# Spreading the fp8 matmuls of a q-k product over a step, and turning inverse norms into a row by way of DRAM

## The chip, the cores and the metric

One core of one Trainium2 chip. The metric is the device time of one execution in microseconds (us); medians over several runs are quoted. The kernel before takes 815.4 us.

Engines: PE is TensorE's matmuls, PEld its weight loads, DVE is VectorE, ACT is ScalarE, POOL is GpSimd, SP is SyncE. L12 is line 12 of the kernel in question.

## The reference

```python
B, N, C = 4, 6016, 256
qn = q / (norm(q, axis=1) + 1e-6)             # over N, one norm for each of 256 columns
kn = k / (norm(k, axis=1) + 1e-6)
a  = softmax(kn.T @ qn / tau, axis=-1)        # 256 x 256 for each of 4 batches
x  = (v @ a).reshape(B * N, 256)
out = (silu(x @ w_gate) * (x @ w_val)) @ w_out     # 24064 tokens, 256 -> 1536 -> 256
```

The kernel folds `a` into the two large weights (Wg, Wv: 256 x 1536 a batch), so that the tokens need three products only: g, v and o.

## The kernel before

Its main loop has 576 steps: 4 batches of 12 chunks of 512 tokens (the last of 384), each with 12 slices of 128 hidden columns. A step puts two matmuls of 512 columns into g, two into v and four of 256 columns into o. During the steps of one batch, the attention of the next is prepared in the background, by a plan that says what is added at which of 144 steps.

```python
    def gemm1_pair(b, t):                      # two slabs of 128 rows of q and k
        ...
        for jh in range(CH):                   # CH = 2
            js = slice(jh * P, (jh + 1) * P)
            if pm == 2:
                nc.tensor.matmul(kq[:, jh, :], q_sb[:, ps:ps + 2, js],
                                 k_sb[:, ps:ps + 2, :], ..., perf_mode=DR)
            else:                              # the 47th slab stands alone
                nc.tensor.matmul(kq[:, jh, :], q_sb[:, ps, js], k_sb[:, ps, :], ...)
    ...
    def norm_cols(b):
        ...                                    # column sums, then inverse norms in inv
        parts = split3(inv[:, CH:], [P, CH], "ink")      # three bf16 parts
        ...
    def norm_diag(b):                          # six diagonal matrices, on DVE
        ...
    def norm_rows(b):                          # ones x diagonal = a row on every partition
        for i in range(3):
            nc.tensor.matmul(ps, ones_bf, state[b, "diag"][:, i], start=(i == 0), stop=(i == 2))
        ink = work.tile([P, C], FP32, tag="ink")
        nc.vector.tensor_copy(ink, ps)
    ...
    def logits(b, jh):                         # DVE: kq * inverse norm of q * row of k
        ...
    plan[step + 1].append((gemm1_pair, t))     # both fp8 matmuls at the end of a step
    ...
    plan[S1 + 10].append((norm_cols,))         # S1 = 82
    plan[S1 + 20].append((norm_diag,))
    plan[S1 + 22].append((norm_rows,))
    plan[S1 + 24].append((logits, 0))
```

DoubleRow (`DR`) multiplies two fp8 slabs at once. The first batch is prepared before the loop, in another way that the change doesn't touch.

## Time and profile before

| | before |
|---|---|
| median of 3 runs | 815.44 us (815.43 to 816.31) |
| span of the profiled run | 813.6 us |
| PE busy | 98% |
| DVE, ACT, POOL busy | 65%, 53%, 33% |
| clock granted to TensorE | 1.0 |

The span starts with the first instruction, so it is a little shorter than the time. A matmul's record overlaps the next one's (one of 512 columns is recorded as 0.38 us, and the next starts 0.216 us after it), so busy shares hide small losses. The distance between the starts of successive g products (the length of a step) does not, and the argument rests on it. The lines stand in the prediction.

### The profile page before, as it was taken

How to read it: one execution, taken by the hardware profiler on the slowest of the kernel's cores; microseconds unless marked ns; L12 is line 12 of the kernel's file. 1: busy time of each engine (PE TensorE's matmuls, PEld its weight loads, DVE VectorE, ACT ScalarE, POOL GpSimd, SP SyncE). 2: the span in 40 equal slices, each digit the busy share in tenths (PEclk: the TensorE clock that was granted, in tenths of full speed). 3: DMA queues.
4: the chain of work that ended last, by engine and by line, in shares of the span. 5: the costliest groups of instructions: out<-in, count | busy, mean ns of one | idle time of the engine just before them, and what ended most of it. 6: DMA issues, size and time to landing. Idle time of an engine off the chain costs nothing.

```text
span 813.6 us, 13772 instructions
## 1 busy us (share of the span) xinstructions
PE 800.4 (98%) x5037; PEld 487.1 (60%) x5037; DVE 526.7 (65%) x816; ACT 434.9 (53%) x756; POOL 265.8 (33%) x344
## 2 busy tenths in 40 slices
PE   5999999999999999999999999999999999999998
PEld 3656666665565666666565666666656565665666
DVE  4777777667556777756756687765765555555554
ACT  4566655545555656545555556654554544444543
POOL 5515887313000888722000388751300000000000
PEclk9999999999999999999999999999999999999999
DMA  9993875328311678333812368632652112112101
GB/s 88 143 158 69 112 105 88 78 53 122 80 40 46 96 100 105 74 65 88 127 40 59 53 87 118 92 78 66 141 97 66 46 48 57 53 39 65 50 27 59
DMA packets 93220, 64.59 MB, mean 79 GB/s; under 512 B 52593, under 2 KB 92017, under 8 KB 92401
## 3 DMA queue, kind: packets, MB, share of 16 engines
q0 software_dynamic: 19200, 27.01, 28.6%
q1 hardware_dynamic: 73952, 36.71, 17.7%
q8 instruction: 39, 0.64, 0.3%
q14 instruction: 29, 0.23, 0.1%
HBM read 78.64 MB, written 36.70 MB: 142 GB/s over the span
## 4 chain that ended last, share of the span: by engine, by line
PE 95%; DMA 4%; POOL 1%; issue 0%; DVE 0%; POOLq 0%
PE o_new L463 30%; PE g_ps L429 30%; PE v_ps L429 30%; PE ps L398 2%; PE kq_new L149 2%; DMA v_sb<-in_v_dram 1%; DMA k_sb<-in_k_dram 1%; DMA q_sb<-in_q_dram 1%; POOL k_sb L104 1%; PE ps L331 0%; PE unit_ps L398 0%; PE cs L305 0%; PE kq_new L154 0%; PE ps L388 0%; PE vt_ps L128 0%
## 5 line engine op out<-in xcount | busy, mean ns | idle before, releaser
L439 DVE TENSOR_TENSOR sv<-silu,v_ps 128x512 bf16<-128x512 bf16 (+1 forms) x576 | 388.6, 675 | 263.2 <-ACT silu L435 261.4
L435 ACT ACTIVATE silu<-g_ps 128x512 bf16<-128x512 f32 (+1 forms) x576 | 338.6, 588 | 324.6 <-PE g_ps L429 302.0
L463 PE MATMUL o_new<-w_out_sb,sv 128*128 128x256 bf16 x2256 | 338.3, 273 | 0.0
L429 PE MATMUL g_ps<-vT,Wg 128*128 128x512 bf16 (+1 forms) x1128 | 331.1, 375 | 0.0
L429 PE MATMUL v_ps<-vT,Wv 128*128 128x512 bf16 (+1 forms) x1128 | 330.4, 374 | 0.0
L463 PEld LDWEIGHTS <-sv 128*128 128x128 bf16 x2256 | 220.7, 98 | 140.8
L429 PEld LDWEIGHTS <-Wv 128*128 128x128 bf16 x1152 | 112.7, 98 | 130.8 <-ACT Wv L410 0.2
L281 POOL TENSOR_TENSOR acc_new<-acc_new,sq 128x512 f32<-128x512 f32 x135 | 157.3, 1165 | 43.7 <-DVE sq L271 33.7
L429 PEld LDWEIGHTS <-Wg 128*128 128x128 bf16 x1152 | 106.7, 98 | 27.0 <-ACT Wg L410 0.2
L271 DVE TENSOR_TENSOR sq<-q_sb 128x512 bf16<-128x512 fp8e5 x72 | 63.9, 888 | 0.0
L276 POOL TENSOR_TENSOR acc_new<-sq 128x512 f32<-128x512 bf16 x3 | 3.5, 1152 | 150.7 <-DVE sq L271 150.7
L272 ACT ACTIVATE sq<-k_sb 128x512 bf16<-128x512 fp8e5 x72 | 44.2, 614 | 0.0
L149 PE MATMUL kq_new<-k_sb,q_sb 128*128 128x512 fp8e5 x184 | 40.0, 309 | 0.7 <-DMA q_sb<-in_q_dram 0.7
L472 ACT COPY o_sb<-o_new 128x512 f32<-128x512 f32 x48 | 28.1, 586 | 14.9 <-PE o_new L463 14.5
L474 DVE COPY o_sb<-o_new 128x512 f32<-128x512 f32 (+1 forms) x48 | 31.8, 661 | 3.0 <-PE o_new L463 3.0
L104 POOL DMA_DIRECT2D q_sb<-in_q_dram x48 | 27.0, 562 | 13.3 <-DMA k_sb<-in_k_dram 5.4
L104 POOL DMA_DIRECT2D k_sb<-in_k_dram x48 | 26.0, 549 | 11.3 <-DMA w_out_sb<-in_moe_w_out_dram 5.3
L176 PE MATMUL ss_new<-sq,ones_bf 128*128 128x256 bf16 x83 | 17.6, 351 | 9.0 <-ACT sq L166 8.4
L112 POOL DMA_DIRECT2D vb<-in_v_dram x47 | 24.1, 516 | 5.3 <-DMA vb<-in_v_dram 3.2
L149 PEld LDWEIGHTS <-q_sb 128*128 128x256 fp8e5 x184 | 22.1, 138 | 3.1 <-DMA q_sb<-in_q_dram 2.3
L176 PEld LDWEIGHTS <-ones_bf 128*128 128x128 bf16 x83 | 9.8, 121 | 15.7 <-issue 11.4
L351 POOL TENSOR_SCALAR den<-th 128x512 f32<-128x512 f32 x3 | 1.8, 612 | 51.8 <-ACT th L350 51.8
(93 smaller groups left out, 201.7 us busy)
## 6 DMA issues: line engine op xcount, KB each, us to landing
out_dram<-o_sb SPq DMA_DIRECT2D x92, 256.0 KB, 2.4
vb<-in_v_dram POOLq DMA_DIRECT2D x43, 256.0 KB, 5.4
k_sb<-in_k_dram POOLq DMA_DIRECT2D x44, 128.0 KB, 5.8
q_sb<-in_q_dram POOLq DMA_DIRECT2D x44, 128.0 KB, 5.0
w_out_sb<-in_moe_w_out_dram POOLq DMA_DIRECT2D x1, 768.0 KB, 13.5
vb<-in_v_dram POOLq DMA_DIRECT2D x4, 192.0 KB, 3.5
vT<-vb SPq DMA_TRANSPOSE x47, 3.8
w_gate_sb<-in_moe_w_gate_dram POOLq DMA_DIRECT2D x2, 256.0 KB, 7.3
```

The lines of the kernel that those rows point to most:

```text
L104: nc.gpsimd.dma_start(out=dst[:, gs:gs + gm, :], in_=src[b].rearrange("(p s) c -> p s c", s=NS)[:, gs:gs + gm, :])
L149: nc.tensor.matmul(kq[:, jh, :], q_sb[:, ps:ps + 2, js], k_sb[:, ps:ps + 2, :], start=(t == 0 and jh == 0), stop=last, perf_mode=DR, skip_ ...
L176: nc.tensor.matmul(state[b, "ss", which], ones_bf, sq[:, s, :], start=(t == 0 and s == 0), stop=(t == t_last and s == pm - 1))
L271: nc.vector.tensor_mul(sq[:, :pm, 0, :], q_sb[:, ps:ps + pm, :], q_sb[:, ps:ps + pm, :])
L272: nc.scalar.activation(sq[:, :pm, 1, :], k_sb[:, ps:ps + pm, :], ACT.Square)
L281: nc.gpsimd.tensor_tensor(out=acc, in0=acc, in1=sq[:, s, :, :], op=ALU.add)
L429: nc.tensor.matmul(dst[:, :mv], W[:, kk, fs], vT[:, kk, :mv], start=(kk == 0), stop=(kk == CH - 1))
L435: nc.scalar.activation(silu[:, :mv], g_ps[:, :mv], ACT.Silu)
L439: nc.vector.tensor_mul(sv[:, f, :mv], silu[:, :mv], v_ps[:, :mv])
L463: nc.tensor.matmul(self.o_ps[:, j % 2, :], self.sv[:, f, j * P:(j + 1) * P], w_out_sb[:, f, :], start=(f == 0), stop=(f == FH - 1))
L472: nc.scalar.copy(o_sb[:, :m, :], self.o_ps[:, :m, :])
L474: nc.vector.tensor_copy(o_sb[:, :m, :], self.o_ps[:, :m, :])
```

## The change

Its intent: to put something of 512 columns between the two fp8 matmuls of a pair, so that their long weight loads are hidden, and to take the nine diagonal matmuls off PE.

```diff
-        plan[step + 1].append((gemm1_pair, t))
+        pair_at[step + 1] = t
...
-        for dst, W in ((g_ps, Wg), (v_ps, Wv)):
+        for n, (dst, W) in enumerate(((g_ps, Wg), (v_ps, Wv))):
             for kk in range(CH):
                 nc.tensor.matmul(dst[:, :mv], W[:, kk, fs], vT[:, kk, :mv], ...)
+            if pair is not None:
+                gemm1_pair(b + 1, pair, (n,))
...
-        parts = split3(inv[:, CH:], [P, CH], "ink")
-        ... (norm_diag and norm_rows go)
+        row = dram.tile([C], FP32, tag="ink_row")
+        nc.gpsimd.dma_start(out=row.rearrange("(h p) -> p h", p=P), in_=inv[:, CH:])
         ink = work.tile([P, C], FP32, tag="ink")
-        nc.vector.tensor_copy(ink, ps)
+        nc.gpsimd.dma_start(out=ink, in_=row.partition_broadcast(P))
```

A pair's step now reads g, fp8, v, fp8, o.

More of the change, by code (lines that the diff above doesn't have):

```diff
@@ L135, in evacuate_first_v, with gemm1_pair @@
         nc.vector.tensor_copy(vt_ready[(0, 0)][:, h, :], state["vt_ps"][:, h, :])
-    def gemm1_pair(b, t):
+    def gemm1_pair(b, t, jhs=range(CH)):
         q_sb, k_sb = qk_tiles[b]
-        if t == 0:
+        if t == 0 and 0 in jhs:
             kq_new = psum_kq.tile([P, CH, C], FP32, tag="kq")
@@ L145, in gemm1_pair @@
         last = t == NP - 1
-        for jh in range(CH):
+        for jh in jhs:
             js = slice(jh * P, (jh + 1) * P)
@@ L312, in norm_cols @@
         state[b, "inv"] = inv
-        parts = split3(inv[:, CH:], [P, CH], "ink")
-        scal = work.tile([P, 3, CH], FP32, tag="scal")
-        for i, part in enumerate(parts):
-            nc.gpsimd.tensor_copy(scal[:, i, :], part)
-        state[b, "scal"] = scal
-    def norm_diag(b):
-        scal = state[b, "scal"]
-        diag = work.tile([P, 3, CH, P], BF16, tag="diag")
-        for i in range(3):
-            for h in range(CH):
-                nc.vector.tensor_scalar_mul(diag[:, i, h, :], in0=ident,
-                                            scalar1=scal[:, i, h:h + 1])
-        state[b, "diag"] = diag
-    def norm_rows(b):
-        ps = psum_m.tile([P, C], FP32, tag="misc")
-        for i in range(3):
-            nc.tensor.matmul(ps, ones_bf, state[b, "diag"][:, i], start=(i == 0),
-                             stop=(i == 2))
+        row = dram.tile([C], FP32, tag="ink_row")
+        nc.gpsimd.dma_start(out=row.rearrange("(h p) -> p h", p=P), in_=inv[:, CH:])
         ink = work.tile([P, C], FP32, tag="ink")
-        nc.vector.tensor_copy(ink, ps)
+        nc.gpsimd.dma_start(out=ink, in_=row.partition_broadcast(P))
         state[b, "ink"] = ink
@@ L417, in wp_unit, with gv_matmuls @@
         wp_evacuate(b, u, ps, part, u % 2 == 1 if on_dve is None else on_dve)
-    def gv_matmuls(b, ci, f):
+    def gv_matmuls(b, ci, f, pair=None):
         cs, cm = chunks[ci]
@@ L479 @@
     plan = [[] for _ in range(STEPS)]
+    pair_at = {}
     for g in range(len(groups)):
@@ L489 @@
     plan[S1 + 10].append((norm_cols,))
-    plan[S1 + 20].append((norm_diag,))
-    plan[S1 + 22].append((norm_rows,))
     plan[S1 + 24].append((logits, 0))
@@ L560 @@
         for f in range(FH):
-            g_ps, v_ps, mv = gv_matmuls(b, ci, f)
+            pair = pair_at.get(ci * FH + f) if b + 1 < B else None
+            g_ps, v_ps, mv = gv_matmuls(b, ci, f, pair)
             us = range(2 * f + 2, min(2 * f + 4, len(wp_units))) if gi == 0 else ()
```

## The prediction

> **What bounds the kernel now.** I read the page first: the span, the busy shares, the chain that ended last.
>
> ```profile
> span 813.6 us, 13772 instructions
> PE 800.4 (98%) x5037; PEld 487.1 (60%) x5037; DVE 526.7 (65%) x816; ACT 434.9 (53%) x756; POOL 265.8 (33%) x344
> PE 95%; DMA 4%; POOL 1%; issue 0%; DVE 0%; POOLq 0%
> ```
>
> The first 36 us are loads; after that everything on the chain is PE. A busy PE is not yet a PE at its pace, so I read the timeline of PE next (start, length, work) and took the distance between the g products of successive steps.
>
> ```profile
> 54.13 0.59 PE L429 MATMUL g_ps<-vT,Wg 128*128 128x512 bf16 x2
> ...
> 64.53 0.59 PE L429 MATMUL g_ps<-vT,Wg 128*128 128x512 bf16 x2
> ...
> 67.35 0.61 PE L429 MATMUL g_ps<-vT,Wg 128*128 128x512 bf16 x2
> ...
> 95.22 0.60 PE L429 MATMUL g_ps<-vT,Wg 128*128 128x512 bf16 x2
> ...
> 101.53 0.60 PE L463 MATMUL o_new<-w_out_sb,sv 128*128 128x256 bf16 x4
> 101.88 0.46 PE L149 MATMUL kq_new<-k_sb,q_sb 128*128 128x512 fp8e5 x2
> 102.19 0.61 PE L429 MATMUL g_ps<-vT,Wg 128*128 128x512 bf16 x2
> 102.63 0.59 PE L429 MATMUL v_ps<-vT,Wv 128*128 128x512 bf16 x2
> ```
>
> From 54.13 to 64.53 lie eight steps without q-k work: 10.40/8 = 1.300 us each. A step streams 4 x 512 + 4 x 256 = 3072 columns, so this is 0.42 ns a column with all included: about 0.216 us for a 512-wide matmul and 0.109 us for a 256-wide one. Stepping through the whole timeline, I found no step between 50 us and the end that is longer than what its matmuls add up to, except as told below. So PE is at its pace, nothing it waits for is worth anything, and only two things can move the time: matmuls taken off PE, and columns that cost more than 0.42 ns.
>
> **What the Trainium skill says.** (1) "Perfetto Trace Analysis", section Identifying the Most-Contended Engine, warns that the matmul busy share does not tell the distance to the limit; hence the steps above, and not the 98%. (2) "TensorE: Matmul & The Clock Gate", section Back-to-back issue gap, gives N/2.4 + 2.5 ns, which is 215.8 and 109.2 ns for 512 and 256 columns; the trace agrees (0.216, 0.109). (3) The same page, section Weight-path perf modes, says that DoubleRow fp8 switches the fast weight load off and makes a weight load 72% dearer. The trace has this smaller, 138 against 98 ns (the groups of weight loads, fp8 128x256 against bf16 128x128). (4) "DMA: Bandwidth & Descriptors", section Anatomy of one DMA, gives about 2.0 us fixed for a transfer issued from GpSimd, mostly the receipt of the last byte. The trace shows 2.4 us for the output stores, issued from SyncE, and 5.4 us for the v loads of 256 KB.
>
> **Part 1: the fp8 matmuls.** What does a pair (two DoubleRow matmuls of 256 columns) cost now? From 67.35 to 95.22 are 20 steps with eight pairs: 27.87 - 20 x 1.300 = 1.87 us, 0.234 us a pair. Two 256-wide matmuls at pace are 0.218. Only 0.016 us a pair is excess. So the most that any new place for these matmuls can win is 0.016 us x 69 pairs (three hidden batches of 23 DoubleRow pairs; the 24th is a single slab without DoubleRow) = 1.1 us, 0.14% of the time. Their own columns are not saved by moving them.
>
> Where does the excess sit? The 138 ns weight load, longer than the 109 ns matmul that should hide it, is the first suspect. It is not the culprit. In the timeline of the weight loads:
>
> ```profile
> 100.56 0.21 PEld L429 LDWEIGHTS <-Wg 128*128 128x128 bf16 x2
> ...
> 101.86 0.25 PEld L149 LDWEIGHTS <-q_sb 128*128 128x256 fp8e5 x2
> 102.18 0.12 PEld L429 LDWEIGHTS <-Wg 128*128 128x128 bf16 x2
> ```
>
> In a step without q-k work the first Wg load starts at 100.56, 0.10 us before its matmul (100.66): hidden. The two fp8 loads start at 101.86, behind the last o matmul, and end 0.25 us later; the start times in ns are 101855 for the last o matmul, 102073 for the second fp8 matmul, exactly two slots of 109 later, so the entry into fp8 and the second fp8 load are free. But the Wg load after the pair starts at 102.18, only 0.01 us before its matmul (102.19): it was not pulled ahead of the fp8 matmul in front. From the second fp8 matmul to the second g matmul the 69 DoubleRow pairs take 113 + 227 (or 114 + 226) = 340 ns, where pace is 109 + 216 = 325. The three single-slab pairs without DoubleRow show exactly 109 + 216. So the excess is **15 ns on each exit** from DoubleRow into bf16, and nothing on the entry.
>
> The change puts one fp8 matmul behind g and one behind v. That makes two entries and two exits a pair where there was one of each. If an exit keeps its price, spreading **adds** 69 x 15 ns = 1.04 us. That is the step I chose; it takes for granted that one DoubleRow matmul alone ends as expensively as two, which no pair here shows. The pair also runs some 0.9 us earlier in its step. Its group's loads are issued 13 steps (17 us) before, those of q land in 3.8 to 5.1 us, and no wait appears before the squares of the same data, so nothing new is waited for. v is finished up to 0.11 us later in those steps, but the product on DVE waits for ACT's silu (261.4 of its 263.2 us idle time), not for v.
>
> **Part 2: the row of inverse norms.** It takes off PE, per hidden batch, three 256-wide matmuls:
>
> ```profile
> 178.31 0.59 PE L429 MATMUL g_ps<-vT,Wg 128*128 128x512 bf16 x2
> ...
> 179.62 0.49 PE L331 MATMUL ps<-diag,ones_bf 128*128 128x256 bf16 x3
> 179.94 0.59 PE L429 MATMUL g_ps<-vT,Wg 128*128 128x512 bf16 x2
> ```
>
> The step lasts 179.94 - 178.31 = 1.63 us against 1.300: 0.33 us, three slots of 0.109. Three batches: **0.99 us saved**. It also takes away 18 multiplications on DVE (3.2 us), three copies (1.3 us) and 21 small POOL instructions of 0.19 to 0.20 us (about 4 us). Neither engine holds PE up in those steps, which are at pace to 0.01 us, so these are worth nothing.
>
> It adds a store of 1 KB in 256 pieces of 4 bytes and a load of the row onto 128 partitions, both on POOL's queue, the second waiting for the first. The question is whether the row is there when the logits want it.
>
> ```profile
> 165.98 1.04 POOL L311 TENSOR_TENSOR inv<-inv,minus 128x4 f32<-128x4 f32 x1
> ...
> 168.38 0.61 POOL L112 DMA_DIRECT2D vb<-in_v_dram  x1
> ```
>
> ```profile
> 183.11 0.48 DVE L342 SCALAR_TENSOR_TENSOR s_new<-kq_new,inv,ink 128x256 f32<-128x256 f32 x1
> ```
>
> The inverse is ready at 167.0, the logits begin at 183.1: 16 us. The way through DRAM I estimate, from the durations above, at 0.6 (issue) + 2.4 to 5.4 (landing) + 0.6 + 2.4 to 5.4 = 6 to 12 us. It fits. While POOL waits for the store, the v load behind it (168.38) is held up by some 1 to 4 us. Its data is for a chunk 24 steps, over 30 us, later, and needs 5.4 us for the load and 3.8 us for the transpose: it fits too.
>
> **Sum.** 815.44 + 1.04 - 0.99 = 815.5 us. The two parts cancel. I predict 815.4, shaded by the first rival.
>
> **The rivals.** (a) The spread hides the fp8 weights, which is surely its intent: the excess comes from two fp8 matmuls in a row, and beside a 512-wide matmul it vanishes. Then -1.04 - 0.99, 813.4 us. For it speaks that the load of 138 ns is longer than a 109 ns slot; against it, that the entry costs nothing in the trace and the exit does. I give it one chance in five. A half of it, exits at half price, would give 814.5. (b) The wait for the row takes the place of the matmuls: the 4-byte pieces are so slow that the row lands over 16 us after the inverse, DVE stands at the logits, v's banks are not freed and PE stands. Each us of PE standing counts three times (three batches). A row that holds PE up for 4 us gives 815.5 + 3 x 4 = 827.5 us. Against it speaks the slack of 4 to 10 us; 3%. (c) POOL's wait holds up the v load so long that its transpose, and with it a chunk, is late. It would take about 20 us; 1%. (d) PE no longer at pace for another reason: an exit into a 256-wide o matmul hides less than one into a 512-wide g, say 30 ns more on half of the new exits: 69 x 30 ns = +2.1 us, 817.5 us. One in ten.
>
> **Range and chances.** With (a) and (d) as the likely edges and some tenths of run-to-run spread (the three runs before lie within 0.9 us) the range is 813.2 to 817.2. Two per cent is 16 us: faster by so much would need more than both parts together hold (2.1 us), slower needs (b) or (c). Faster 0.5%, within 2% 97.5%, slower 2%.
>
> **What will show it.** The steps with a pair should last about 1.30 + 0.218 + 0.03 = 1.55 us, all of it in one step, with both bf16 weight loads that follow an fp8 matmul starting only some 0.01 us before their matmul. If those loads start 0.1 us early and the pair costs 0.218, rival (a) is right. The steps at 104 of each batch should be 1.30 us, 0.33 less than now. The row's load should land before 180 us on today's clock, and no wait of DVE's logits for a DMA should be in the chain of waits. What would make me wrong: a stretch in which the g products are further apart than their matmuls add up to, with PE waiting for DVE or a DMA.

## The result and the profile after

The changed kernel takes 815.52 us (median of 6 runs, 815.27 to 816.26) beside 815.43 us (6 runs, 815.32 to 816.31) for the kernel before. The ratio is 1.0001, with a 95% interval of 0.9988 to 1.0014: the same. Ratios are the mean time of one kernel's fast runs over that of the other's of the same rounds, so not quite the ratio of the medians.

The page of the changed kernel:

```profile
span 813.7 us, 13727 instructions
PE 798.7 (98%) x5028; PEld 480.7 (59%) x5028; DVE 519.8 (64%) x795; ACT 434.1 (53%) x756; POOL 264.9 (33%) x329
```

PE has nine matmuls fewer, as intended. That the span did not shrink says nothing yet of why. The timeline of PE around a step with a pair (start, length, what), where L412 is now the line of g and v and L450 that of o:

```profile
65.88 0.59 PE L412 MATMUL g_ps<-vT,Wg 128*128 128x512 bf16 x2
66.12 0.46 PE L149 MATMUL kq_new<-k_sb,q_sb 128*128 128x512 fp8e5 x1
66.42 0.61 PE L412 MATMUL v_ps<-vT,Wv 128*128 128x512 bf16 x2
66.68 0.46 PE L149 MATMUL kq_new<-k_sb,q_sb 128*128 128x512 fp8e5 x1
66.98 0.61 PE L450 MATMUL o_new<-w_out_sb,sv 128*128 128x256 bf16 x4
67.42 0.60 PE L412 MATMUL g_ps<-vT,Wg 128*128 128x512 bf16 x2
```

The step lasts 67.42 - 65.88 = 1.54 us; before, it was 1.52 or 1.53 and the step after it 1.31 where 1.30 is the pace. The 69 steps of this form last 1.548 us on the mean, and the step after each 1.30. The weight loads of the same step:

```profile
66.09 0.14 PEld L149 LDWEIGHTS <-q_sb 128*128 128x256 fp8e5 x1
66.42 0.12 PEld L412 LDWEIGHTS <-Wv 128*128 128x128 bf16 x2 [0.19 <-issue]
66.65 0.14 PEld L149 LDWEIGHTS <-q_sb 128*128 128x256 fp8e5 x1
66.97 0.33 PEld L450 LDWEIGHTS <-sv 128*128 128x128 bf16 x4 [0.19 <-issue]
```

The fp8 load at 66.09 begins as the second g matmul begins (66.092 by the records in ns) and runs beside its 0.216 us: it is hidden. But both bf16 loads behind an fp8 matmul start with the matmul that needs them (66.42 and 66.42; 66.97 and 66.98), and the load path stands idle for 0.19 us before each. The table of waits counts them (who waited for what, us in total, times, longest; "issue" is time in which the engine waited for nothing that the profile shows):

```profile
PEld L412 <- issue: 12.9, 69, 0.2
PEld L450 <- issue: 12.9, 69, 0.2
```

There are 69 of each, two for every DoubleRow pair. By the start times in ns, it is some 329 from the second g matmul to the first v matmul, with the fp8 matmul between, and 227 from there to the second v matmul: 556, where the pace gives 216 + 109 + 216 = 541. From the second v matmul to the first o matmul it is 329 or 330, and 120 to the next: 449 to 450, where the pace gives 216 + 109 + 109 = 434. So each exit costs 15 to 16 ns. (The record of an fp8 matmul itself starts too early to be read so: 28 ns after the matmul ahead of it.)

The step that held the diagonal matmuls, 1.63 us before, is now an ordinary one, 180.01 - 178.71 = 1.30 us:

```profile
178.71 0.59 PE L412 MATMUL g_ps<-vT,Wg 128*128 128x512 bf16 x2
...
180.01 0.59 PE L412 MATMUL g_ps<-vT,Wg 128*128 128x512 bf16 x2
```

The way through DRAM took longer than predicted. In the list of transfers (size, median us from issue to landing) and in DVE's timeline of the third batch:

```profile
row<-inv POOLq DMA_DIRECT2D x3, 1.0 KB, 9.4
```

```profile
572.47 0.69 DVE L426 TENSOR_TENSOR sv<-silu,v_ps 128x512 bf16<-128x512 bf16 x1 [0.84 <-ACT silu L422]
573.08 0.48 DVE L325 SCALAR_TENSOR_TENSOR s_new<-kq_new,inv,ink 128x256 f32<-128x256 f32 x1
```

The store of 1 KB lands 9.4 us after its issue (8.6 and 10.7 in the other batches). The inverse is ready at 167.4, 362.2 and 557.1 us, and the row lands at 181.6, 377.3 and 572.5: 14.2, 15.1 and 15.4 us later. DVE begins the logits at 183.17, 378.01 and 573.08, so the row was there 1.6, 0.7 and 0.6 us ahead. In the third batch the product just before the logits starts at 572.47, as the row lands (572.48), after 0.84 us of idle time in place of the usual 0.61. It looks as if the row had held DVE up, and the expectation of e2 below takes it so. The record says otherwise: in e9, where the row landed at 564.31, DVE's timeline shows the same pause in the same place (and in e8 too, 0.84 us, with the row there at 566.23):

```profile
572.81 0.69 DVE L428 TENSOR_TENSOR sv<-silu,v_ps 128x512 bf16<-128x512 bf16 x1 [0.83 <-ACT silu L424]
```

So the row held nothing up in the changed kernel; the cause of this pause of 0.23 us is not shown. PE's steps there are still 1.30 us. POOL's next v load came at 178.00 where it was 168.38 before, without harm; 0.4 us of this is the later schedule (inverse ready at 167.4, not 167.0).

### The profile page after: what moved, and what is told of

It is laid out like the page before. It is cut to its first block, busy times and chain, and to the rows that moved or that the text cites. A ratio compares the mean times of both kernels' runs of the same rounds, so it can differ in the third digit from the quotient of the medians.

```text
span 813.7 us, 13727 instructions
## 1 busy us (share of the span) xinstructions
PE 798.7 (98%) x5028; PEld 480.7 (59%) x5028; DVE 519.8 (64%) x795; ACT 434.1 (53%) x756; POOL 264.9 (33%) x329
## 4 chain that ended last, share of the span: by engine, by line
PE 95%; DMA 4%; POOL 1%; issue 0%; DVE 0%; POOLq 0%
PE o_new L450 30%; PE v_ps L412 30%; PE g_ps L412 30%; PE ps L381 2%; PE kq_new L149 2%; DMA v_sb<-in_v_dram 1%; DMA k_sb<-in_k_dram 1%; DMA q_sb<-in_q_dram 1%; POOL k_sb L104 1%; PE unit_ps L381 0%; PE cs L305 0%; PE kq_new L154 0%; PE ps L371 0%; PE vt_ps L128 0%; DVE o_sb L461 0%
## 5 line engine op out<-in xcount | busy, mean ns | idle before, releaser
L450 PE MATMUL o_new<-w_out_sb,sv 128*128 128x256 bf16 x2256 | 339.2, 273 | 0.0
L412 PE MATMUL v_ps<-vT,Wv 128*128 128x512 bf16 (+1 forms) x1128 | 331.5, 376 | 0.0
L412 PE MATMUL g_ps<-vT,Wg 128*128 128x512 bf16 (+1 forms) x1128 | 330.5, 375 | 0.0
L450 PEld LDWEIGHTS <-sv 128*128 128x128 bf16 x2256 | 214.8, 98 | 137.4 <-issue 12.9
L412 PEld LDWEIGHTS <-Wv 128*128 128x128 bf16 x1152 | 107.0, 98 | 127.4 <-issue 12.9
L412 PEld LDWEIGHTS <-Wg 128*128 128x128 bf16 x1152 | 112.0, 98 | 23.2 <-ACT Wg L393 0.2
L149 PE MATMUL kq_new<-k_sb,q_sb 128*128 128x512 fp8e5 x184 | 71.1, 417 | 0.7 <-DMA q_sb<-in_q_dram 0.7
L271 DVE TENSOR_TENSOR sq<-q_sb 128x512 bf16<-128x512 fp8e5 x72 | 60.6, 841 | 0.0
L176 PE MATMUL ss_new<-sq,ones_bf 128*128 128x256 bf16 x83 | 15.5, 317 | 10.8 <-ACT sq L166 10.1
L309 POOL TENSOR_TENSOR inv<-inv,half 128x4 f32<-128x4 f32 x3 | 3.1, 1035 | 37.1 <-DVE inv L308 37.1
```

Source lines behind the costliest of these rows:

```text
L149: nc.tensor.matmul(kq[:, jh, :], q_sb[:, ps:ps + 2, js], k_sb[:, ps:ps + 2, :], start=(t == 0 and jh == 0), stop=last, perf_mode=DR, skip_ ...
L176: nc.tensor.matmul(state[b, "ss", which], ones_bf, sq[:, s, :], start=(t == 0 and s == 0), stop=(t == t_last and s == pm - 1))
L271: nc.vector.tensor_mul(sq[:, :pm, 0, :], q_sb[:, ps:ps + pm, :], q_sb[:, ps:ps + pm, :])
L412: nc.tensor.matmul(dst[:, :mv], W[:, kk, fs], vT[:, kk, :mv], start=(kk == 0), stop=(kk == CH - 1))
L450: nc.tensor.matmul(self.o_ps[:, j % 2, :], self.sv[:, f, j * P:(j + 1) * P], w_out_sb[:, f, :], start=(f == 0), stop=(f == FH - 1))
```

## The experiments

For changes of about 1 us, I use besides the time the **stretch** from the start of the first g product to that of the g product of the last step but one, both read from the timeline of PE. It leaves out the loads at the beginning, whose length differs between executions (the first g product starts at 38.0 to 39.1 us in these traces).

| kernel | exits from DoubleRow | diagonal matmuls | time us (before, same rounds) | stretch us |
|---|---|---|---|---|
| before | 69 | 9 | 815.43 | 804.17 - 38.36 = 765.81 |
| after | 138 | 0 | 815.52 (815.43) | 804.26 - 38.41 = 765.85 |
| e1_spread_only | 138 | 9 | 816.44 (815.41) | 805.30 - 38.47 = 766.83 |
| e2_row_only | 69 | 0 | 814.12 (815.41) | 802.82 - 38.00 = 764.82 |
| e3_four_exits | 276 | 0 | 817.70 (815.41) | 806.46 - 38.19 = 768.27 |
| e5_bundle_4 | 18 | 0 | 813.51 (815.63) | 802.28 - 38.22 = 764.06 |
| e4_bundle_all | 3 | 0 | 813.42 (815.41) | 802.24 - 38.42 = 763.82 |

My theory: the two parts of the change are of opposite sign and nearly equal, 15 ns for each exit from DoubleRow against 0.109 us for each matmul removed. The first rival: the spread wins, and something else (the row) takes it back.

### Each part alone

e1 is the kernel before with the spread alone. e2 is the changed kernel with this put back:

```diff
-        pair_at[step + 1] = t
+        plan[step + 1].append((gemm1_pair, t))
```

> The kernel before with the fp8 matmuls spread and nothing else; the diagonal matmuls stay. Theory (15 ns for each exit from DoubleRow into bf16, two exits a pair instead of one): 69 x 15 ns = 1.04 us more than before, about 816.5 us; in the profile a step with a pair lasts 1.55 us and is followed by one of 1.30, and the step with the diagonal matmuls still lasts 1.63 us. Rival (the spread hides the fp8 weight loads, and something else in the change cost what it won): 1.0 us less than before, 814.4 us, steps with a pair of 1.52 us.

> The changed kernel with the fp8 matmuls back in pairs at the end of a step; the row still goes by way of DRAM. Theory (nine matmuls of 0.109 us leave PE and nothing waits for the row): 0.99 us less than before, about 814.45 us; the step with the diagonal matmuls falls from 1.63 to 1.30 us, steps with a pair are back at 1.52 followed by 1.31. Rival (the row's late landing, which held DVE up by 0.2 us in the third batch of the changed kernel, costs PE some of it): between 814.5 and 815.4 us, with a step near the logits longer than 1.30 us.

Measured: e1 816.44 us (5 runs, 816.27 to 816.55), ratio 1.0010 (0.9996 to 1.0024). The interval alone leaves room for no change; the stretch is longer by 1.02 us, against 1.04 expected. Its step with diagonal matmuls lasts 1.63 us:

```profile
178.76 0.59 PE L429 MATMUL g_ps<-vT,Wg 128*128 128x512 bf16 x2
...
180.06 0.49 PE L331 MATMUL ps<-diag,ones_bf 128*128 128x256 bf16 x3
180.39 0.59 PE L429 MATMUL g_ps<-vT,Wg 128*128 128x512 bf16 x2
```

e2 814.12 us (5 runs, 814.06 to 814.53), ratio 0.9984 (0.9972 to 0.9997). Its stretch is shorter by 0.99 us, as expected; the other 0.3 us of the medians' difference lie before the first g product (38.00 against 38.36 us in the traces), so they are hardly the change's. The rival falls: the spread alone makes the kernel slower, the row alone makes it faster, and the two sum to what was measured: 1.02 - 0.99 = 0.03 us, where the changed kernel's stretch is longer by 0.04.

### More exits

Each DoubleRow matmul is cut into two of 128 columns, one behind each of the four matmuls of g and v.

```diff
             for kk in range(CH):
                 nc.tensor.matmul(dst[:, :mv], W[:, kk, fs], vT[:, kk, :mv], ...)
+                if pair is not None and pairs[pair][1] == 2:
+                    gemm1_pair(b + 1, pair, (n,), kk)      # columns kk * 128 to kk * 128 + 127
```

(The single slab stays as in the changed kernel.)

> The changed kernel with every DoubleRow matmul cut into two of 128 columns, one behind each of the four g and v matmuls: four exits a pair where the changed kernel has two, and as many columns. Theory: 69 x 2 x 15 ns = 2.07 us for the exits and 69 x 2 x about 2 ns = 0.3 us for the fixed part of two more matmuls, so about 2.4 us more than the changed kernel, 817.9 us, and a pair's step of about 1.58 us. Rival (the price is one of the fp8 weight load of 137 ns, which now stands behind a slot of 216 ns each time and is hidden): no more than the 0.3 us, 815.8 us. If the exit's price depends on the length of the fp8 matmul in front (half a slot is waited for), it lies between.

Measured: 817.70 us (5 runs, 817.52 to 818.69), ratio 1.0031 (1.0018 to 1.0043). The stretch is 2.42 us longer than the changed kernel's; 2.4 was expected. Spread over 138 more exits this is 17.5 ns each, of which about 2 are the fixed part of one more matmul (an estimate: 2 x 109 - 216 ns). From one v matmul to the next, with an fp8 matmul of half the width between, are 287 ns in the trace; the v matmul's own 216 and some 56 for 128 columns (an estimate, on the straight line through 109 and 216 ns) leave 15. So the price is the same behind 128 columns of fp8 as behind 256, and hiding the fp8 load behind 512 columns does not remove it.

### Fewer exits

The row by way of DRAM, and the pairs collected: 24 (e4) or 4 (e5) at a time. The diff is shown against e2.

```diff
-        plan[step + 1].append((gemm1_pair, t))
+        if (t + 1) % 24 == 0 or t == NP - 1:               # e5: 4 in place of 24
+            for u in range(t // 24 * 24, t + 1):
+                plan[step + 1].append((gemm1_pair, u))
```

> The row by way of DRAM, and all 24 pairs of a batch in one burst at the end of the step where the last of them stood: one exit a batch from DoubleRow, or none, as the burst ends with the single slab that needs no DoubleRow. Theory: against the row alone 69 x 15 ns = 1.04 us less, so about 813.4 us, 2.0 us less than before and 2.1 less than the changed kernel. Rival (a burst of 48 x 0.109 = 5.2 us starves ACT and DVE, and PE then waits for them): the step after the burst shows PE idle, and the gain is gone, 814.5 us or more.

> The row by way of DRAM and the fp8 matmuls in bursts of four pairs, 0.87 us each: six bursts a batch, the last of which ends with the single slab, so 5 exits from DoubleRow a batch in place of 23. Theory: against the kernel with pairs and the row, 3 x 18 x 15 ns = 0.8 us less, and against the one with a single burst 15 x 15 ns = 0.2 us more: from the first g product to the last some 764.0 us, where these two have 764.8 and 763.8. The time about 813.5 us. Rival (what the single burst won has another cause than the exits): nearer to 764.8.

Measured: e4 813.42 us (5 runs, 813.17 to 813.62), ratio 0.9974 (0.9961 to 0.9986); e5 813.51 us (5 runs, 813.36 to 813.65), ratio 0.9973 (0.9961 to 0.9986). Both beat both kernels, by some 2 us. The timeline of PE in e4:

```profile
139.98 0.59 PE L412 MATMUL g_ps<-vT,Wg 128*128 128x512 bf16 x2
...
141.20 5.26 PE L149 MATMUL kq_new<-k_sb,q_sb 128*128 128x512 fp8e5 x46
146.31 0.39 PE L154 MATMUL kq_new<-k_sb,q_sb 128*128 128x256 fp8e5 x2
146.54 0.59 PE L412 MATMUL g_ps<-vT,Wg 128*128 128x512 bf16 x2
...
147.84 0.59 PE L412 MATMUL g_ps<-vT,Wg 128*128 128x512 bf16 x2
```

The burst's step lasts 146.54 - 139.98 = 6.56 us, which is 1.300 + 48 x 0.109 = 6.53 and one exit, to about 0.01; the next step is 1.30 us. ACT stands idle for 5.96 us and DVE for 5.19 around the burst, and PE doesn't wait for them afterwards, so their idle time cost nothing here. The burst has one exit, from DoubleRow into the single fp8 slab: its three matmuls take 223 + 120 = 343 ns where three slots of 109 are 327. The price is therefore one of leaving DoubleRow, not of leaving fp8, and e5 has six exits a batch, not the five that I had counted. From 69 exits to 18 the stretch falls by 0.76 us (14.9 ns each), and from 18 to 3 by 0.24 us (16 ns each).

### How near the row came to the path

In the changed kernel with the column sums four steps later:

```diff
-    plan[S1 + 10].append((norm_cols,))
+    plan[S1 + 14].append((norm_cols,))
```

> The changed kernel with the column sums of the norms four steps (5.2 us) later and the logits where they were. In the changed kernel the row landed 14.2, 15.1 and 15.4 us after the inverse was ready, and DVE's work at the logits was due 15.2 us after it; now it is due 10.0 us after it. Theory (rival (b) of the prediction was nearly true: only a margin of some tenths of a us kept the row off the path): DVE is held up for 4.2 to 5.4 us in each batch, PE can run on for 1.0 to 1.8 us until it needs the v bank, so PE stands some 3 us in each of the three batches: 9 to 12 us more than the changed kernel, 825 to 828 us. Rival (there is more slack than that, in buffers or in a store that lands sooner when it starts later): under 2 us more, below 817.5 us.

Measured: 822.74 us (4 runs, 821.38 to 823.88), ratio 1.0087 (1.0072 to 1.0102). That is 7.2 us more than the kernel before (815.52 in these rounds; the changed kernel's median is 815.52 too), not 9 to 12, but far over the rival's 2. The row landed 14.0, 13.8 and 13.7 us after the inverse, a little sooner than in the changed kernel, and DVE stood for 3.4, 3.3 and 2.9 us, less than the 4.2 to 5.4 us expected. The expectation had also set DVE's need too early: 15.2 us after the inverse comes the product ahead of the logits, the logits themselves at 15.8 to 16.0. Of the first batch, DVE's timeline, then that of PE:

```profile
186.75 0.48 DVE L325 SCALAR_TENSOR_TENSOR s_new<-kq_new,inv,ink 128x256 f32<-128x256 f32 x1 [3.43 <-DMA ink<-row]
```

```profile
185.27 0.59 PE L412 MATMUL g_ps<-vT,Wg 128*128 128x512 bf16 x2
187.88 0.59 PE L412 MATMUL v_ps<-vT,Wv 128*128 128x512 bf16 x2 [2.02 <-DVE sv L426]
...
188.75 0.99 PE L412 MATMUL g_ps<-vT,Wg 128*128 128x512 bf16 x2
189.53 1.06 PE L412 MATMUL v_ps<-vT,Wv 128*128 128x512 bf16 x2
```

PE waits 2.02 us for DVE to free the v bank, the buffer that the v product is summed in (1.88 and 1.68 us in the other batches, 5.6 us in all). In this batch a second cost follows: the g and v products at 188.75 and 189.53 are 0.78 us apart and not 0.43, because the granted clock fell to a half, from 188.81 to 192.22 us (`--windows 188.81:192.22` gives 0.50). The profiled execution is the slowest of the four (823.88 us, a span 8.4 us longer than the changed kernel's): the three steps with the waits are 2.18, 2.04 and 1.84 us over their 1.30, the two steps after the first of them 1.19 and 0.49 us at the lower clock, the ones after the others 0.3 us each, 8.3 us together. The table of stretches has it (stretch; its length, busy us of PE, PEld, DVE, ACT and POOL; then the clock, DMA's share and GB/s). Its 0.73 is the mean of full and half clock over those 4 us:

```profile
183.00:187.00 4.00, 2.86 (x18) 1.57 (x16) 0.57 (x2) 1.19 (x2) 0.00 (x0) 1.00 0.54 98
187.00:191.00 4.00, 3.12 (x13) 1.59 (x13) 3.40 (x7) 1.60 (x3) 1.42 (x3) 0.73 0.46 118
```

The margin of the changed kernel was thus real but thin: 0.6 to 1.6 us, about a step, until DVE stands. Until PE stands there are another 1.2 to 1.4 us (what DVE stood here less what PE then waited).

### Why the store is slow

Three variants of the changed kernel: both transfers issued from SP (e7); the store as 128 pieces of 8 bytes, which permutes the row (e8); the store as one piece of 1 KB that holds a constant (e9).

```diff
-        nc.gpsimd.dma_start(out=row.rearrange("(h p) -> p h", p=P), in_=inv[:, CH:])
+        nc.sync.dma_start(out=row.rearrange("(h p) -> p h", p=P), in_=inv[:, CH:])      # e7, the load too
+        nc.gpsimd.dma_start(out=row.rearrange("(p h) -> p h", h=CH), in_=inv[:, CH:])   # e8
+        nc.gpsimd.dma_start(out=row.rearrange("(o c) -> o c", o=1), in_=flat)           # e9
```

(`flat`: a row on one partition, filled with 0.129.)

> The changed kernel with the store and the load of the row issued from SyncE and not from POOL. Theory A (the 256 pieces of 4 bytes are slow to be confirmed, whoever issues them): the store lands 7 to 10 us after its issue as before. Theory B (POOL's software queue is the slow part): it lands in 2 to 3 us, as the output stores do. The time of the kernel stays that of the changed kernel either way, 815.5 us, unless SyncE's wait holds up an output store or a transpose.

> The row stored in another order, as 128 pieces of 8 bytes in place of 256 of 4 bytes, otherwise as the changed kernel; the row is then permuted and the result is wrong on purpose. If the store's landing goes by the number of pieces, it falls from 8.6 to 10.7 us to about 5 to 6 us; if it is a fixed latency, it stays at about 9. The time is that of the changed kernel.

> The row stored as one piece of 1 KB from one partition that holds a constant near the true inverse norms, after the inverse is ready; the result is wrong on purpose, if only slightly. If the pieces make the store slow it lands within about 3 us of its issue; if any store to DRAM from POOL followed by a wait takes as long, about 9 us. The time is that of the changed kernel.

Measured, in the list of transfers of e7, e8 and e9 in this order:

```profile
row<-inv SPq DMA_DIRECT2D x3, 1.0 KB, 10.0
```

```profile
row<-inv POOLq DMA_DIRECT2D x3, 1.0 KB, 3.5
```

```profile
row<-flat POOLq DMA_DIRECT2D x3, 1.0 KB, 1.6
```

The times are 815.54 us (4 runs), 815.53 us (one run) and 815.84 us (one run): as the changed kernel, as expected. The issuing queue makes no clear difference (9.2 to 11.8 us from SP, 8.6 to 10.7 from POOL, three stores each). The shape of the pieces does: the same 1 KB takes 9.4, 3.5 and 1.6 us in 256, 128 and 1 pieces. The fall to 3.5 is more than the halved count explains, so the size of 4 bytes, or the order of the addresses, matters as well; these runs don't tell those apart. e9 also reads from one partition and not from 128. The pieces are those of the program: on POOL's queue the trace records each of the three stores as 16 packets of 64 bytes. Those of the slow store are done within 0.2 us (169.14 to 169.33 us); the landing is then reported by one DMA engine after the other between 173.4 and 177.1 us. What happens in between is not seen. e8 and e9 were wrong, yet their results passed the comparison: the 256 norms are so nearly alike that it can't see a permuted or constant row. That comparison is no evidence that the row is in the right order.

### A version with room for the row

e4 with the column sums four steps earlier (`S1 + 6`).

> The kernel with one burst a batch, and the column sums of the norms four steps (5.2 us) earlier, so that the row has some 5 us to spare before the logits. Theory: nothing on PE changes, so the same time as with the single burst, 813.4 us, but the row lands about 5 us or more before DVE needs it, and no execution in which the store takes 12 us costs anything. It should beat both kernels by 2.0 us. Rival (POOL or the row's transfers now meet something that they did not meet): a wait of PE in steps 88 to 100 and more than 814 us.

Measured: 813.54 us (5 runs, 813.26 to 814.12), ratio 0.9972 (0.9959 to 0.9986). The stretch is 802.85 - 39.12 = 763.73 us, as e4's, and past 50 us no step is longer than in e4, but for the one of the column sums, which has moved by four. The profiled execution is the slowest of the five; its clock was at a half from 34.35 to 37.76 us, before the first g product. The row lands at 176.0, 370.8 and 563.8 us; DVE begins the logits at 183.1, 377.3 and 571.7. That leaves 7.1, 6.4 and 7.9 us. It is as fast as e4 within the noise, and a store as slow as the slowest here (11.8 us, in e7) would still land in time.

## Why the prediction was right, point by point

- **What bounds the kernel: right.** Past 50 us every step of the changed kernel is again as long as its matmuls and exits; nothing that DVE, ACT or POOL were spared showed in the time. The formula in point (2) of the prediction is given in that section for a single isolated matmul; here it holds in a stream of weight loads and matmuls (216 and 109 ns).
- **The excess of a pair sits on the exit, not on the fp8 load: right.** Shown by e1 (+1.02 us), e3, e4 and e5. The step taken for granted, that a single DoubleRow matmul ends as expensively as two, held: 15 to 16 ns at each exit. Why the load isn't pulled ahead there remains open, and so does why a load of 98 ns that starts 4 ns ahead of its matmul (66.417 and 66.421 us) costs no more than 15.
- **Nine matmuls, 0.99 us: right.** e2 shows 0.99 us.
- **The sum: right, and by its own terms.** Predicted +1.04 - 0.99 = +0.05 us; the stretch grew by 0.04, the median by 0.09. The time of 815.4 was shaded by rival (a) from 815.5; 815.52 was measured. A total of about nothing would also fit a change without effect; it is e1 and e2 that show the two terms.
- **Rival (a): wrong.** The spread alone costs 1.02 us. **Rival (d): wrong.** An exit into the 256-wide o matmul costs no more than one into a 512-wide one.
- **The way through DRAM: mis-sized.** The step that failed is the estimate of 6 to 12 us, whose first landing was taken as 2.4 to 5.4 us from transfers with much larger pieces. The store took 8.6 to 10.7 us and the whole way 14.2 to 15.4. "The row's load should land before 180 us" was wrong (181.6), as was the v load's delay of 1 to 4 us (over 9). That the row fits was right, but with 0.6 to 1.6 us to spare before DVE needs it and not 4 to 10: this part came out right by luck. Rival (b), at 3%, was nearer than that. It was right that PE would then stand once in each of three batches: 2.02, 1.88 and 1.68 us in the profiled execution of e6.

## What to carry to other kernels

Where PE is at pace, read the lengths of equal steps from the timeline, take off the columns at pace, and price what is left: it tells in advance how much a rearrangement can win. Here only 16 ns a pair were to be had, and they belonged to leaving DoubleRow, so here such matmuls were better in few bursts than between others. A change of two parts whose sum is zero is worth taking apart: keeping the row and bundling the pairs won 2 us. A small store in 4-byte pieces that something waits for needs its own measured latency and a margin in the plan.

## What the Trainium skill lacked or had wrong

- "TensorE: Matmul & The Clock Gate", section Weight-path perf modes: it does not say that the weight load behind a DoubleRow matmul is not pulled ahead. The runs show 15 to 16 ns at each exit, into bf16 and into single-slab fp8 alike, and nothing at the entry. It gives 72% for the dearer DoubleRow weight load; the groups here show 138 against 98 ns, 41%. Its Part 1, on the HAM clock gate, has the clock fall to 4/8 after an idle window of about 3.4 us. In e6 it fell to a half for 3.41 us, but PE had stood for 2.02 us only and was busy for 1.39 of the 3.41 us before (185.40 to 188.81); after waits of 1.88 and 1.68 us it did not fall.
- "DMA: Bandwidth & Descriptors", section Anatomy of one DMA: about 2.0 us fixed; a store of one 1 KB piece took 1.6 us here, somewhat less. Of a store to DRAM in tiny pieces the page gives no latency: 3.3 to 3.5 us for 128 of 8 bytes, and for 256 of 4 bytes 7.5 to 10.7 us over all runs that issue it from POOL.
